# One VectorE sum moved behind four folding operations, ahead of the first output pair of a state-space plus gated-MLP kernel

## The chip, the cores and the metric

The kernel runs on one core of one Trainium2 chip. The time is device microseconds of one execution, and the figure of a kernel is the median over its runs. The core's engines work side by side, each through its own queue of instructions in order: TensorE (PE for its matmuls, PEld for its weight loads), VectorE (DVE), ScalarE (ACT), GpSimd (POOL) and SyncE (SP, which here only issues transfers). An instruction waits at the head of its queue until what it needs is there, and all that stands behind it on that engine waits too.

## The reference

The input `x` is one sequence of 2048 tokens of width 512. It is normalised over its width (`xn`), and two branches read `xn`. Branch A is a diagonal complex state-space layer with 512 states: a projection into the states, a recurrence over all tokens, a projection back, and a skip term. Branch B is a gated MLP with 1792 inner columns. The output is `x` plus both.

```python
xn = layernorm(x)
# A: Bu = xn @ B_bar.T ; h_t = Lam_bar * h_(t-1) + Bu_t
#    y = 2 * Re(h @ C.T) + xn * Dskip
# B: out = (silu(xn @ w1) * (xn @ w3)) @ w2
return x + A(xn) + B(xn)
```

All tensors are bfloat16. Nothing in the change alters what is computed.

## The kernel before

**Tiling.** The 2048 tokens are four blocks of 512. For each block `glu(b)` makes the 14 gate and up products of the MLP (L525), ScalarE takes them out of PSUM (L534, L535), VectorE multiplies them (L543); `bu(b)` makes the inputs of the recurrence (L435), and `ssm_tasks(b)` turns, scans and turns back the states on VectorE (L457 to L488), with two additions per half done by accumulating transfers that GpSimd issues (L468, L492). All of it lands in one activation tile per block, `act`.

**Output pairs.** The last product, `act` by the stacked weights `w2` and `C`, is done for two 128-token chunks at a time, in `y_fast(n)`, n from 0 to 7. Each pair is a two-by-two block product of seven multiplications in place of eight (Strassen's scheme in Winograd's form), so that sums of blocks are needed beforehand: of the activations, `S1 = a21 + a22`, `S3 = a11 - a21` (in place of a21) and `S2 = S1 - a11`, made by `row_sums` (all on L683), and `S4 = a12 - S2`, made inside `y_fast` (L766); of the weights, the eight differences of `weight_sums` (L662), made once.

**PE's order in a pair.** Seven groups of 11 matmuls, all on L724: a11, then S1, then a12, then S2, then a22, then S4, then S3. S4 overwrites a12, so L766 waits for the third group, and the sixth group waits for L766.

**Where the sums lie.** For the pairs 0, 2, 4 and 6, S1 goes over the storage of `x_blk[0]` and S2 over that of `x_blk[1]` (`sum_homes`). So S1 has to wait until block 0 of `x` is no longer read, and S2 until block 1 is no longer read. The last reader of `x_blk[b]` is a transfer: `res_tasks(b)` multiplies `xn_blk[b]` by the skip vector (L622) and then has GpSimd issue an accumulating transfer `xn_blk[b] += x_blk[b]` (L626).

**C's folding.** `weight_c(pt)` multiplies the complex C by the discretisation factor, for four groups of states. Groups 0 and 1 end with one subtraction on VectorE (L400). Groups 2 and 3 end with two fused operations each (L397), which read products that ScalarE made shortly before (L386). The weight differences (L662) read the folded C.

**What sets VectorE's order.** The background work of VectorE is a list, `bg`, a `Filler`. `bg.add(cost, fn, key)` appends a task; `fill`, called after each group of matmuls while the program is written out, takes tasks from the front as long as an estimated VectorE time stays near an estimated PE time; `flush(key)` takes tasks until the last one with that key is out. The order in the list is the order in VectorE's queue, with the gate products (L543) set in between. The list ahead of the first pair is written at L812 to L825: residual of block 0, three weight differences, residual of block 1, folding of groups 0 and 1, a difference of the residual (L634), the three row sums, folding of groups 2 and 3, five weight differences. `ssm_tasks(1)` then adds the turning of block 1, and `y_fast(0)` begins after `glu(1)`.

**After the first pair.** `y_fast(1)` follows at once, and then `glu(2)`, whose matmuls need `xnT` of block 2. That is made by ScalarE (sums L269, squares L275, normalisation L285) with three small steps on GpSimd between them (L272; L278 to L280), and four transposing transfers that SP issues (L242).

Of the kernel before, what the change touches and what calls it, by code (L numbers as in the profile page):

```python
# [63 lines left out]
def kernel(  # L64
# [141 lines left out]
    bg = Filler(LEAD)  # L206
# [207 lines left out]
    def act(b):  # L414
        if act_blk[b] is None:
            act_blk[b] = actp.tile([P, 2 * NK, TBLK], FP16, name="act")
        return act_blk[b]
# [213 lines left out]
    def res_difference(b):  # L631
        def difference():
            o = xn_blk[b]
            nc.vector.tensor_tensor(out=o[:, 0::2, D2].bitcast(FP16), in0=o[:, 0::2, D2], in1=o[:, 1::2, D2],  # L634
                                    op=ALU.subtract)

        bg.add(0.4, difference, ("res", b))
# [38 lines left out]
    def row_sums(n, b, p):  # L676
        a = act(b)
        r1, r2 = slice(2 * p * P, (2 * p + 1) * P), slice((2 * p + 1) * P, (2 * p + 2) * P)
        a11, a12 = a[:, 0:NK, r1], a[:, NK:2 * NK, r1]
        a21, a22 = a[:, 0:NK, r2], a[:, NK:2 * NK, r2]  # L680
        s1, s2 = (v.bitcast(FP16).rearrange("p (k t) -> p k t", t=P) for v in homes[n % 2])
        sums[n] = dict(a11=a11, a12=a12, a22=a22, s1=s1, s2=s2, s3=a21)
        return [(0.9, lambda out=out, x=x, z=z, op=op: nc.vector.tensor_tensor(out=out, in0=x, in1=z, op=op), ("sums", n))  # L683
                for out, x, z, op in ((s1, a21, a22, ALU.add), (a21, a11, a21, ALU.subtract),
                                      (s2, s1, a11, ALU.subtract))]
# [123 lines left out]
    pairs = [(b, p) for b in range(NBLK) for p in range(CPB // 2)]  # L809
# [7 lines left out]
    for fn in finish_c[:2]:  # L817
        bg.add(0.7, fn, "tw")
    res_difference(0)
    for t in row_sums(0, *pairs[0]):  # L820
        bg.add(*t)
    for fn in finish_c[2:]:
        bg.add(1.4, fn, "tw")
    for i, which in ((0, 3), (1, 2), (1, 0), (1, 1), (1, 3)):
        weight_sum(i, which)  # L825

# [70 lines left out]
```

## Time and profile before

| What | Value |
|---|---|
| median of 8 runs | 206.22 us (205.59 to 207.2) |
| the profiled execution: its time | 205.59 us |
| the profiled execution: its span | 203.8 us, so 1.8 us lie around the span |
| PE granted clock, whole span | 0.999 |
| VectorE busy, 61.2 to 63.1 us | 0.02 us of 1.9 |
| PE busy, 60 to 70 us | 9.95 us of 10 |
| PE busy, 70 to 77 us | 6.15 us of 7 |
| PE busy, 77 to 88 us | 10.83 us of 11 |
| L626 for block 1 | issued at 58.12 us, landed 5.0 us later |
| L626, all four | 4.5 to 6.4 us from issue to landing |

Times in the profile count from the start of the span. A row of the timeline gives the start, the length, the engine, the line, the operation and its operands; in square brackets stands how long the engine had been idle and what ended the idle time. Consecutive VectorE operations overlap by some 0.08 us, so that the step from one start to the next is a little shorter than the length shown. The chain of waits follows the work that ended last backwards: a piece of PE in it is time in which PE was the limit, a piece of VectorE is time in which PE's next work hung on VectorE.

### The profile page before, as it was taken

Reading aid. Unit: us, or ns where it says so; the run is one execution under the profiler, and the core shown is the slowest. Engines: PE = TensorE matmul, PEld = TensorE weight load, DVE = VectorE, ACT = ScalarE, POOL = GpSimd, SP = SyncE. Lnnn points to the kernel's source line nnn. Section 1 sums busy time; section 2 is a strip of 40 time slices with the busy share of each in tenths; the row PEclk is TensorE's granted clock in tenths of the full one; section 3 lists DMA queues with packets and bytes.
Section 4 is the critical chain, followed back from the end, with each engine's and each line's share of the span. In section 5 each row is a group of like instructions: output and inputs, shape, how many; then the busy total and the mean of one; then the engine's idle time right before and its main releaser. Section 6 shows DMA issues by size and latency. Waiting matters only on the chain.

```text
span 203.8 us, 3431 instructions
## 1 busy us (share of the span) xinstructions
PE 197.9 (97%) x1304; PEld 122.5 (60%) x1317; DVE 172.6 (85%) x242; ACT 125.0 (61%) x251; POOL 41.7 (20%) x65
## 2 busy tenths in 40 slices
PE   8999999999999998999999999999999999999994
PEld 2774444444444587854444445888444458888993
DVE  3789699999996999999959999999999935684932
ACT  4699797799999966588876676210566672101010
POOL 3250279600310141434111010310101210000000
PEclk9999999999999999999999999999999999999999
DMA  6998994991672015844796105476240790101011
GB/s 167 271 278 193 329 158 102 332 279 37 123 149 40 0 37 97 156 126 91 94 179 132 26 0 106 83 150 132 77 77 0 142 169 2 51 3 51 26 43 39
DMA packets 28696, 23.16 MB, mean 114 GB/s; under 512 B 16008, under 2 KB 26376, under 8 KB 28680
## 3 DMA queue, kind: packets, MB, share of 16 engines
q1 hardware_dynamic: 25512, 13.21, 26.5%
q0 software_dynamic: 2592, 9.44, 24.8%
q10 hardware_dynamic: 576, 0.30, 0.5%
q8 instruction: 10, 0.16, 0.3%
q14 instruction: 6, 0.05, 0.1%
HBM read 7.74 MB, written 2.10 MB: 48 GB/s over the span
## 4 chain that ended last, share of the span: by engine, by line
PE 86%; DVE 7%; DMA 4%; issue 0%; ACTq 0%; ACT 0%
PE gu_ps L525 41%; PE gu_ps L724 16%; PE y_ps L724 8%; PE y_ps L435 7%; PE bu_ps L435 7%; PE bu_ps L724 6%; DMA w_sb<-in_B_w_dram 2%; DMA x_blk<-in_A_x_dram 1%; DVE tw L662 1%; DVE ct L397 1%; DVE act L543 1%; DVE p L457 1%; PE gu_ps L557 1%; PE bu_ps L557 1%; DVE u L461 1%; DVE xn L735 1%
## 5 line engine op out<-in xcount | busy, mean ns | idle before, releaser
L525 PE MATMUL gu_ps<-xnT,w_sb 128*128 128x512 bf16 x415 | 91.9, 379 | 0.5
L525 PEld LDWEIGHTS <-w_sb 128*128 128x128 bf16 x424 | 41.5, 98 | 49.4
L724 PEld LDWEIGHTS <-act 128*128 128x128 f16 x451 | 43.2, 98 | 6.8 <-DVE act L766 1.3
L534 ACT ACTIVATE g<-gu_ps 128x512 bf16<-128x512 f32 x55 | 33.1, 601 | 13.2 <-PE gu_ps L525 12.9
L535 ACT ACTIVATE u<-gu_ps 128x512 bf16<-128x512 f32 x55 | 33.2, 603 | 9.6 <-PE gu_ps L525 9.2
L543 DVE TENSOR_TENSOR act<-g,u 128x1024 f16<-128x1024 bf16 x28 | 19.0, 678 | 3.9 <-ACT u L535 3.9
L435 PEld LDWEIGHTS <-bt 128*128 128x128 bf16 x128 | 12.5, 98 | 15.1
L478 DVE TENSOR_TENSOR_SCAN u<-rho,act,u 128x512 bf16<-128x512 f32 x16 | 19.6, 1268 | 0.0
L492 POOL DMA_DIRECT2D act<-p x8 | 7.2, 900 | 42.2 <-DVE act L488 28.2
L435 PE MATMUL y_ps<-xnT,bt 128*128 128x512 bf16 x63 | 15.1, 379 | 0.1
L435 PE MATMUL bu_ps<-xnT,bt 128*128 128x512 bf16 x61 | 14.8, 379 | 0.1
L457 DVE TENSOR_TENSOR p<-u,tabe 128x2048 bf16<-128x2048 bf16 x8 | 9.8, 1221 | 2.6 <-DMA act<-p 2.5
L468 POOL DMA_DIRECT2D u<-p x6 | 5.3, 878 | 30.0 <-DVE u L461 9.9
L724 PE MATMUL y_ps<-tw,act 128*128 128x256 f16 x88 | 10.9, 273 | 0.0
L724 PE MATMUL gu_ps<-w_sb,act 128*128 128x256 bf16 (+1 forms) x84 | 10.8, 268 | 0.0
L724 PE MATMUL gu_ps<-tw,act 128*128 128x256 f16 x88 | 10.7, 273 | 0.0
L437 ACT ACTIVATE u<-bu_ps 128x512 bf16<-128x512 f32 x16 | 9.4, 597 | 2.0 <-PE bu_ps L435 1.6
L437 ACT ACTIVATE u<-y_ps 128x512 bf16<-128x512 f32 x16 | 9.5, 596 | 1.8 <-PE y_ps L435 1.3
L461 DVE TENSOR_TENSOR u<-u,tabe 128x2048 bf16<-128x2048 bf16 x8 | 9.8, 1222 | 0.2
L744 ACT ACTIVATE bu_ps<-y_ps 128x256 f32<-128x256 f32 x4 | 1.5, 369 | 13.7 <-PE y_ps L724 13.7
L478 DVE TENSOR_TENSOR_SCAN u<-rho,ends,u 128x512 bf16<-128x512 f32 x8 | 9.9, 1267 | 0.0
L484 DVE TENSOR_TENSOR p<-u,tabe 128x2048 f16<-128x2048 bf16 x8 | 9.8, 1222 | 0.1
(143 smaller groups left out, 277.2 us busy)
## 6 DMA issues: line engine op xcount, KB each, us to landing
act<-p POOLq DMA_DIRECT2D x8, 512.0 KB, 4.8
u<-p POOLq DMA_DIRECT2D x6, 512.0 KB, 4.7
xn<-x_blk POOLq DMA_DIRECT2D x4, 512.0 KB, 5.5
out_dram<-xn SPq DMA_DIRECT2D x15, 128.0 KB, 1.7
w_sb<-in_B_w_dram SPq DMA_DIRECT2D x1, 1792.0 KB
x_blk<-in_A_x_dram SPq DMA_DIRECT2D x3, 512.0 KB, 9.3
w_sb<-in_B_w_dram SPq DMA_DIRECT2D x2, 768.0 KB, 6.8
w_sb<-in_B_w_dram SPq DMA_DIRECT2D x4, 256.0 KB, 4.2
```

The source lines that it names most:

```text
L435: nc.tensor.matmul(out=ps, lhsT=bt[:, ri, dt, pt * P:(pt + 1) * P], rhs=xnT_blk[b][:, dt, :], start=(dt == 0), stop=(dt == NDT - 1))
L437: nc.scalar.activation(out=u[:, j, ri, :], in_=ps, func=ACT.Copy)
L457: nc.vector.tensor_tensor(out=st["p"][:, :, ::-1, :], in0=st["g"], in1=tabe[:, psl, 2:0:-1, :], op=ALU.mult)
L461: nc.vector.tensor_tensor(out=st["g"], in0=st["g"], in1=tabe[:, psl, 0:1, :].to_broadcast(FULL), op=ALU.mult)
L478: nc.vector.tensor_tensor_scan(out=v, data0=rho[:, pt:pt + 1].to_broadcast([P, TBLK]), data1=v, initial=init, op0=ALU.mult, op1=ALU.add)
L484: nc.vector.tensor_tensor(out=st["p16"][:, :, ::-1, :], in0=st["g"], in1=tabe[:, psl, 1:3, :], op=ALU.mult)
L492: gp.dma_start(out=act_state(b, hf), in_=st["p16"], accum_op=ALU.add)
L525: nc.tensor.matmul(out=ps[:, tsl], lhsT=w[:, dt, f * P:(f + 1) * P], rhs=xnT[:, dt, tsl], start=(dt == 0), stop=(dt == NDT - 1))
L534: nc.scalar.activation(out=g16[:, f % 2, :], in_=g_ps, func=ACT.Silu)
L535: nc.scalar.activation(out=u16[:, f % 2, :], in_=u_ps, func=ACT.Copy)
L543: nc.vector.tensor_tensor(out=act(b)[:, k0:k1 + 1:k1 - k0, :], in0=g16, in1=u16, op=ALU.mult)
L724: nc.tensor.matmul(out=out, lhsT=left[:, k, :], rhs=right[k][:, cols], start=(start and k == 0), stop=(k == NK - 1), skip_group_check=True)
```

## The change

The third row sum, S2, is added to the list after the folding of groups 2 and 3, and not before it. S1 and S3 keep their place. In VectorE's queue the four L397 operations move ahead of the last L683 operation of pair 0; the queues of the other four engines hold the same instructions in the same order.

```diff
     for fn in finish_c[:2]:
         bg.add(0.7, fn, "tw")
     res_difference(0)
-    for t in row_sums(0, *pairs[0]):
+    first_sums = row_sums(0, *pairs[0])
+    for t in first_sums[:2]:
         bg.add(*t)
     for fn in finish_c[2:]:
         bg.add(1.4, fn, "tw")
+    bg.add(*first_sums[2])
     for i, which in ((0, 3), (1, 2), (1, 0), (1, 1), (1, 3)):
         weight_sum(i, which)
```

## The prediction

> **What bounds the kernel now.** I read the engine totals first, then the chain of waits, then the waits of VectorE and PE in the stretch that the diff touches, and last the timelines there.
>
> ```profile
> PE 197.9 (97%) x1304; PEld 122.5 (60%) x1317; DVE 172.6 (85%) x242; ACT 125.0 (61%) x251; POOL 41.7 (20%) x65
> ```
>
> PE is busy 97% of the span, so a change on another engine counts only where PE stands still for it. The chain shows one such place after the start-up:
>
> ```profile
> 63.90 2.73 DVE ct L397 x4
> 66.64 1.00 DVE tw L662
> ...
> 75.63 0.60 DVE act L543
> 76.23 0.08 DVE ends L833
> 76.31 0.81 DVE act L766
> 77.12 0.05 issue
> 77.17 1.38 PE bu_ps L724 x11
> 78.54 1.20 PE y_ps L724 x11
> 79.74 8.41 PE gu_ps L724 x77
> ```
>
> From 63.90 to 77.12 the chain runs through VectorE alone, one operation after the other, and ends in L766, which makes S4 for the first pair; then it is PE's again, and from 77.17 on it stays with PE until 199.58. PE's own rows show what the wait cost it:
>
> ```profile
> 73.58 1.36 PE L724 MATMUL y_ps<-tw,x_blk 128*128 128x256 f16 x11
> 74.78 1.36 PE L724 MATMUL y_ps<-tw,act 128*128 128x256 f16 x11
> 77.17 0.94 PE L724 MATMUL bu_ps<-w_sb,act 128*128 128x256 bf16 x7 [1.02 <-DVE act L766]
> ```
>
> A group of 11 takes 74.78 - 73.58 = 1.20 us, so the sixth group was due at 74.78 + 1.20 = 75.98 and began at 77.17: PE lost 1.19 us. (The idle figure of 1.02 counts from the modelled end of the last matmul.) VectorE, which was late there, had itself stood still once:
>
> ```profile
> 60.32 0.89 DVE L683 TENSOR_TENSOR act<-act 128x1408 f16<-128x1408 f16 x1
> 63.09 0.89 DVE L683 TENSOR_TENSOR x_blk<-x_blk,act 128x1408 f16<-128x1408 f16 x1 [1.88 <-DMA xn<-x_blk]
> 63.90 2.73 DVE L397 SCALAR_TENSOR_TENSOR ct<-ct,w2c,tw 128x512 f16<-128x512 bf16 x4
> 66.55 1.09 DVE L662 TENSOR_TENSOR tw<-w_sb,tw 128x1792 f16<-128x1792 bf16 x1
> ```
>
> S2 (63.09) waited 1.88 us for the transfer `xn += x` of block 1, which still read the storage that S2 takes. No other VectorE wait lies between 40 and 90 us, so this idle time arrives whole at L766.
>
> **The change part by part.** No instruction is added or removed. Four L397 operations pass one L683; no queue of PE, ACT, POOL or SP changes.
>
> *The L397 operations, earlier.* S3 starts at 60.32 and the next start could follow 0.81 us later (the step from 63.09 to 63.90), at 61.13. What must be there: the products of ScalarE, whose last L386 starts at 60.31 and takes 0.71, so ends at 61.02 for the last of them, and for the third and fourth L397 only; and `w2c`, long made. No wait. The four take 66.55 - 63.90 = 2.65 us and end at 63.78.
>
> *S2, later.* The transfer was issued at 58.12 and let S2 start at 63.09. Nothing ahead of its issue changes. At 63.78 it has landed, with 0.69 us to spare. S2 then takes 0.81 and L662, at 66.55 before, starts at 64.59: VectorE is 1.96 us earlier. Bounds for the landing from the four L626 rows, 4.5 to 6.4 us after issue: 62.6 to 64.5. At the late end S2 waits 0.7 us and VectorE is 1.2 us earlier. I take the row of this very transfer, 63.09.
>
> *From L662 to L766.* Thirteen operations that follow each other with hardly a gap now. Each could meet a new wait once it comes 1.96 us earlier. Of the four gate products L543 the first was made ready before 60 us; those at 70.21, 73.81 and 75.55 need ScalarE's L535, which end at 63.87, 67.33 and 70.78; they would start at 68.25, 71.85 and 73.59: no wait. L766 needs PE's third group, whose last matmuls start at 73.15 and run 0.60, to 73.75; it would start at 76.23 - 1.96 = 74.27: no wait, 0.5 us to spare. It would end at 77.11 - 1.96 = 75.15, ahead of PE's due time of 75.98. So PE's wait goes altogether, and the gain there is the smaller of 1.96 and 1.19: **1.19 us**. Were VectorE only 1.2 us earlier, it would still be about 1.2.
>
> *What is late next.* Two things. First, `glu(2)`: PE comes to it at 87.98 - 1.19 = 86.79, and needs all four transposes of block 2. SP issues the fourth at 82.82 and is held until 84.57; its 256-byte packets end at about 87.2. Between 84 and 86 the transfers of the software queue alone moved (48 and 50 packets, the accumulation L468 that GpSimd issued at 82.06); the transposes' packets came after it, 435 of the hardware queue from 86 to 87.
>
> ```profile
> 82.06 0.93 POOL L468 DMA_DIRECT2D u<-p  x1 [4.64 <-DVE u L461]
> 82.82 1.75 SPq L242 DMA_TRANSPOSE xnT<-xn  x1
> 87.98 2.32 PE L525 MATMUL gu_ps<-xnT,w_sb 128*128 128x512 bf16 x9
> ```
>
> Both chains move. GpSimd's L278 began at 75.16, behind an L468 of VectorE's making (74.19 to 75.08); that L468 comes 1.9 us earlier, and then ScalarE's last sum, at 74.15, decides: L278 starts about 0.95 us earlier, and so do L279, L280, L285 and the transposes. The second L468 hangs on VectorE and comes 1.9 us earlier: its packets, 83.5 to 86.7 before, lie at 81.6 to 84.8 and now meet the third transpose too. If third and fourth both follow the accumulation, with about 0.9 us of packets each (as the third had, 82.5 to 83.5) they end near 84.8 + 1.8 = 86.6; unhindered the fourth would end about 84.4 (2.5 us from issue, like the second and third, at 81.87). Both are before 86.79. I take no wait; the bounds are 0 and 0.4 us (nothing of the chain moves, 87.2).
>
> The DMA page of the Trainium skill (DMA: Bandwidth & Descriptors, Queues, rings and completion order) says that an engine takes its queues in turn, packet by packet; the rows from 84 to 86 show one queue alone. By the rule the transposes end near 84.4 to 85, by the rows near 86.6, and the sum is the same.
>
> A rule against the change is in the page SBUF — State Buffer (Who interferes with whom): a VectorE instruction with two SBUF inputs and a GpSimd instruction that reads SBUF block each other. L278 to L280 move under other VectorE operations; here they took 0.53, 1.37 and 0.20 us, the same steps for block 3 took 0.79, 2.09 and 0.21. With the longer rows the transposes gain nothing, the fourth ends near 87.2 and 0.4 of the 1.19 is lost.
>
> Second, pair 2: its L766 runs from 130.88 to 131.76, and PE's sixth group begins at 131.97. That margin is 0.2 us. It stays, since VectorE is tied to PE again at 88.19, where its addition of pair 1 waits for PE's last group: in the first pairs VectorE may run 1.96 ahead, but from there on both are 1.19 earlier.
>
> *Sum.* Span 203.8 - 1.19 = 202.6; with the 1.8 us around it the profiled execution goes from 205.59 to 204.4. That execution was the fastest of the eight; the median is 0.63 above it, so I set the gain against the median: 206.22 - 1.2 = **205.0 us**. Own range of this case, 204.5 to 205.5: the gain between 0.7 and 1.7, the upper end because PE may have lost more in the slower runs.
>
> **The rivals.**
>
> *A, transposes late.* The wait removed comes back in part at `glu(2)`: 0.4 us if the last transpose still ends at 87.2. For it: the accumulation now covers two transposes. Against it: the chain ahead of them starts earlier. 206.22 - 0.8 = 205.4.
>
> *B, the change doesn't do what it says.* S2 still waits, because the transfer lands late in most runs. Half the gain is left if VectorE is only 0.6 us earlier, that is a landing at about 65.1, 7.0 us after issue. Against it: the L626 rows end at 6.4. For it: one accumulation of this size (L492 at 38.3) took 9.4. 206.22 - 0.6 = 205.6; with none left 206.2.
>
> *C, slower.* Place: the first matmul of `glu(2)`. Third and fourth transpose both stand still until the accumulation ends at 84.8 and then run one after the other at the longest unhindered time of issue to landing, 2.9 us each: 90.6, a wait of 3.8 in place of 1.19, so 206.22 + 2.6 = 208.8. It is slower by more than 0.3% from a landing at 86.79 + 1.19 + 0.62 = 88.6 on. Against it: the first three followed each other at 1.3 us, not 2.9.
>
> **How the numbers follow.** My forecast 0.67, A 0.15, B 0.10, C 0.08. The predicted time is the forecast's, 205.0. The range takes in the forecast, A and most of B: 204.3 to 206.1. A measurement of this kernel can tell a change of about 0.3%, 0.62 us, from none. Faster by more: 0.65 from the forecast, 0.09 from A, 0.01 from B, together 0.75. Within: 0.02, 0.06 and 0.08, together 0.16. Slower: C and a part of B, 0.09.
>
> **What would show it.** In the changed profile: the four L397 start near 61.1 with no idle time before them; L683 follows near 63.8 with no wait for the transfer; L766 ends near 75.2; PE's sixth group starts at 76.0 with no idle time; `glu(2)` starts near 86.8. The forecast is wrong if VectorE still waits there by more than 0.7 us, if PE waits before `glu(2)`, or if pair 2's sixth group waits for its L766.

## The result, and the profile after

The changed kernel takes 204.12 us in the median of 11 runs (203.69 to 205.2), against 206.27 us for the kernel before in 32 runs (205.2 to 207.96). The ratio is 0.9901 with a 95% interval of 0.9882 to 0.9920: it is 1.6 to 2.4 us faster, where 1.2 was forecast. The direction and the place were right; the gain came out larger, and the time lies 0.2 us below the range. The profiled execution took 204.66 us with a span of 202.4; the span is 1.4 less than before, the time 0.9 less, since 2.3 us lie around this span and 1.8 lay around that one.

The timeline of VectorE after (start, length, engine, line, operation; an idle time would stand in brackets at the end):

```profile
59.97 0.89 DVE L683 TENSOR_TENSOR act<-act 128x1408 f16<-128x1408 f16 x1
60.78 2.73 DVE L397 SCALAR_TENSOR_TENSOR ct<-ct,w2c,tw 128x512 f16<-128x512 bf16 x4
63.55 0.89 DVE L683 TENSOR_TENSOR x_blk<-x_blk,act 128x1408 f16<-128x1408 f16 x1
64.36 1.08 DVE L662 TENSOR_TENSOR tw<-w_sb,tw 128x1792 f16<-128x1792 bf16 x1
...
74.03 0.88 DVE L766 TENSOR_TENSOR act<-act,x_blk 128x1408 f16<-128x1408 f16 x1
```

The four L397 follow S3 at once, S2 has no bracket, and the step from S3 to L766 is 14.06 us where it was 15.91 (60.32 to 76.23): 1.85 less, forecast 1.96. PE's timeline after:

```profile
73.36 1.36 PE L724 MATMUL y_ps<-tw,x_blk 128*128 128x256 f16 x11
74.56 1.36 PE L724 MATMUL y_ps<-tw,act 128*128 128x256 f16 x11
75.76 0.93 PE L724 MATMUL bu_ps<-w_sb,act 128*128 128x256 bf16 x7
```

The sixth group follows the fifth after 1.20 us, like the fifth the fourth: nothing is lost. L766 ended at 74.91 (74.03 + 0.88), 0.85 us ahead of it. The chain of waits after, in the stretch where it ran through VectorE before:

```profile
67.17 2.75 PE gu_ps L525 x12
69.92 1.20 PE y_ps L724 x11
71.12 2.40 PE bu_ps L724 x22
73.52 2.40 PE y_ps L724 x22
75.92 1.20 PE bu_ps L724 x11
77.12 1.20 PE y_ps L724 x11
78.32 8.41 PE gu_ps L724 x77
86.73 0.22 PE gu_ps L525
```

It is PE's all the way. What is left of VectorE's lead is given back in the second pair, where VectorE now waits for PE (its waits between 63 and 100 us):

```profile
DVE x_blk L735 <- PE gu_ps L724: 0.5, 1, 0.5
DVE act L766 <- PE gu_ps L724: 0.2, 1, 0.2
```

So the 1.85 us of VectorE became 1.19 us of PE, as forecast, and the rest is idle time of VectorE. In this pair of profiles that explains 1.2 of the 1.4 us of span. The medians differ by 2.15, and the experiments are about that difference.

One figure recurs below. PE's first full-width matmul of `glu(0)` (L525) starts between 12.41 and 13.57 us in the profiles, whatever the kernel, where the chain of waits before it runs through the first loads of `x` and the weights. I call the time from there to the end of the span "the rest": it is 190.80 us in the profile before and 189.62 in the profile after, a difference of 1.18, which agrees with PE's 1.19 lost. Spans are shown to 0.1 us, so a rest is known to 0.05. The other 0.22 of the span's 1.4 lies in that start.

### The profile page after: what moved, and what is told of

Same layout as the page of the kernel before. It is cut to its first block, busy times and chain, and to the rows that moved or that the text cites. A ratio compares the mean times of both kernels' runs of the same rounds, so it can differ in the third digit from the quotient of the medians.

```text
span 202.4 us, 3431 instructions
## 1 busy us (share of the span) xinstructions
PE 196.9 (97%) x1304; PEld 122.4 (60%) x1317; DVE 172.7 (85%) x242; ACT 125.4 (62%) x251; POOL 40.3 (20%) x65
## 4 chain that ended last, share of the span: by engine, by line
PE 93%; DMA 2%; SPq 2%; DVE 1%; issue 1%
PE gu_ps L525 45%; PE gu_ps L724 16%; PE y_ps L724 9%; PE bu_ps L724 7%; PE y_ps L435 7%; PE bu_ps L435 7%; DMA w_sb<-in_B_w_dram 2%; PE gu_ps L557 1%; PE bu_ps L557 1%; DVE xn L735 1%; SPq L166 0%; SPq L151 0%; SPq L161 0%; SPq L152 0%; DVE x_blk L735 0%
## 5 line engine op out<-in xcount | busy, mean ns | idle before, releaser
L525 PE MATMUL gu_ps<-xnT,w_sb 128*128 128x512 bf16 x415 | 91.9, 379 | 0.5
L525 PEld LDWEIGHTS <-w_sb 128*128 128x128 bf16 x424 | 41.4, 98 | 49.4
L484 DVE TENSOR_TENSOR p<-u,tabe 128x2048 f16<-128x2048 bf16 x8 | 9.8, 1220 | 0.1
```

The costliest lines, as they stand in the source:

```text
L484: nc.vector.tensor_tensor(out=st["p16"][:, :, ::-1, :], in0=st["g"], in1=tabe[:, psl, 1:3, :], op=ALU.mult)
L525: nc.tensor.matmul(out=ps[:, tsl], lhsT=w[:, dt, f * P:(f + 1) * P], rhs=xnT[:, dt, tsl], start=(dt == 0), stop=(dt == NDT - 1))
```

## The experiments

Theory 1: PE loses more to the wait in most runs than in the one profile of before, and the wait is the whole cause. Theory 2: the wait costs 1.2 us, and the order brings something elsewhere. Later expectations name two more. All kernels of one batch share a chip and the runs of the kernel before on it.

### The kernel before, profiled again

No edit. What was expected of the first two:

> The kernel before, unchanged, profiled once more. Theory 1 (the wait is longer in most runs than in the one profile of before, since the transfer of L626 for block 1 lands later): S2 on L683 waits 2.3 to 4 us in place of 1.88, the landing is 5.5 to 7 us after issue in place of 5.0, and PE's sixth group of the first pair starts 1.6 to 3 us late in place of 1.19. Theory 2 (the wait in that profile is typical, and the rest of the 2.15 us is won elsewhere): wait 1.7 to 2.1 us, sixth group 1.0 to 1.4 us late, and a second place where PE stands still that the first profile does not have.

> The kernel before, unchanged, a third profile. Theory 1: wait at S2 2.3 to 4 us, the sixth group of the first pair 1.6 to 3 us late. Theory 2: wait 1.7 to 2.1 us, sixth group 1.0 to 1.4 us late.

Waiting row and PE row of the first of them:

```profile
63.16 0.89 DVE L683 TENSOR_TENSOR x_blk<-x_blk,act 128x1408 f16<-128x1408 f16 x1 [2.49 <-DMA xn<-x_blk]
...
77.23 0.94 PE L724 MATMUL bu_ps<-w_sb,act 128*128 128x256 bf16 x7 [1.52 <-DVE act L766]
```

Together with two more looks on another chip (their expectations stand further down) and the profile of the prediction:

| Profile of before | landing of L626 after issue | S2 waits | sixth group late | `glu(2)` late | the rest |
|---|---|---|---|---|---|
| the one forecast from | 5.0 | 1.88 | 1.19 | 0.00 | 190.80 |
| look_before_1 | 5.5 | 2.49 | 1.69 | 0.01 | 191.34 |
| look_before_2 | 5.2 | 2.04 | 1.38 | 0.14 | 191.13 |
| look_before_3 | 5.1 | 2.19 | 1.38 | 0.23 | 191.19 |
| look_before_4 | 5.2 | 2.08 | 1.43 | 0.00 | 191.05 |

(Microseconds; late is the start of the sixth group less the start of the fifth less 1.20, and the start of `glu(2)` less the start of the last group of the second pair less 1.20.) In all five the sixth group starts 14.07 or 14.08 us after S2 does (63.16 and 77.23 above), so what S2 loses to the landing PE loses one for one. Theory 1 has the direction, though of the four only look_before_1 reaches the sizes that it first named, and look_before_2 lies within theory 2's: the profile forecast from had the earliest landing, the shortest wait and the smallest loss of the five. The mean loss is 1.41 us.

Theory 2 needs a second place where PE stands still. There is one in two of the five, at the start of `glu(2)`, where the weight loads wait for a transpose of block 2. In look_before_3:

```profile
86.39 1.36 PE L724 MATMUL gu_ps<-tw,act 128*128 128x256 f16 x11
87.82 2.55 PE L525 MATMUL gu_ps<-xnT,w_sb 128*128 128x512 bf16 x10
87.82 2.27 PEld L525 LDWEIGHTS <-w_sb 128*128 128x128 bf16 x12 [0.35 <-DMA xnT<-xn]
```

The mean over the five is 0.08 us, so it explains little of the 2.15. It is absent in the three profiles of the changed kernel and in the three without the transfer below.

### The cause taken away: no transfer to wait for

```diff
         def add():
-            gp.dma_start(out=xn_blk[b], in_=x_blk[b], accum_op=ALU.add)
+            if b != 1:
+                gp.dma_start(out=xn_blk[b], in_=x_blk[b], accum_op=ALU.add)
```

In the order of before, and so with nothing for S2 to wait for.

> Order of before, without the accumulating transfer of block 1 (the output of block 1 lacks x). So S2 has nothing to wait for, and the order of VectorE is as it was. Theory 1: all of the gain comes from this wait, so the time is that of the changed kernel, 204.1 (203.7 to 204.6), ratio to before 0.988 to 0.992. Theory 2: only 1.2 us, 205.1 (204.8 to 205.4), ratio 0.993 to 0.996.

204.37 us against 205.75 of before on that chip (ratio 0.9931, 0.9905 to 0.9956): 1.4 us. The times that the expectation names, 204.1 and 205.1, come from the first measurement, so I compare the ratio: it lies above theory 1's band (0.988 to 0.992) and just inside theory 2's. By itself this run does not decide between them; the next ones on one chip do. Its rest is 189.59 us, that of the changed kernel within the 0.05 to which it is known. S2 follows S3 at once in the old order:

```profile
60.75 0.89 DVE L684 TENSOR_TENSOR act<-act 128x1408 f16<-128x1408 f16 x1
61.56 0.88 DVE L684 TENSOR_TENSOR x_blk<-x_blk,act 128x1408 f16<-128x1408 f16 x1
62.36 2.73 DVE L397 SCALAR_TENSOR_TENSOR ct<-ct,w2c,tw 128x512 f16<-128x512 bf16 x4
```

### The lead given back by fixed work

The changed kernel, with six small additions behind S2 (their target is overwritten before it is read):

```diff
     bg.add(*first_sums[2])
+    room = x_blk[0].rearrange("p c d -> p (c d)").bitcast(FP16)
+    for _ in range(6):
+        bg.add(0.0, lambda: nc.vector.tensor_tensor(out=room[:, NK * P:NK * P + D], in0=room[:, 0:D], in1=room[:, D:2 * D], op=ALU.add), "tw")
```

> Order of after, with six additions of 512 elements on VectorE behind S2, some 0.33 us each, so that VectorE reaches L766 2.0 us later by a fixed amount and not by a wait for a transfer. L766 ends 0.9 us ahead of PE's need in the profile of after, so 2.0 - 0.9 = 1.1 us come back. Theory 1: 204.1 + 1.1 = 205.2 (204.9 to 205.6), a full us below before, since the wait in before is longer than 2 us in most runs; sixth group 1.0 to 1.3 us late. Theory 2: what hangs on VectorE's lead elsewhere is lost too, so 205.8 to 206.4.

206.46 us, ratio 1.0029 (1.0002 to 1.0056): hardly slower than before, but 0.9 us above the 205.6 at which theory 1's band ends, so that expectation missed. VectorE's timeline, and then PE's waits between 60 and 143 us:

```profile
64.78 2.71 DVE L828 TENSOR_TENSOR x_blk<-x_blk 128x512 f16<-128x512 f16 x6
```

```profile
PE bu_ps L724 <- DVE act L766: 1.8, 1, 1.8
PE gu_ps L525 <- DMA xnT<-xn: 0.2, 1, 0.2
```

The six take 2.63 us (64.78 to 67.41), not 2.0. PE's sixth group is 1.92 us late, that is 2.63 less 0.71: what L766 has to spare goes first, and the remainder reaches PE. The second line of the waits is the place of rival A of the prediction: PE waits for a transpose of block 2, and `glu(2)` starts 1.55 us after the last group of the second pair where the pace is 1.20, so 0.35 late. Together 2.3 us, as much as the rest grew (191.88 against 189.6); the time is 2.1 above the 204.37 that `no_add` takes on this chip. It is just above theory 2's band, but by the profile this is VectorE's lateness and no second effect of the order.

### The change and the missing transfer on one chip

Four kernels on one chip. `no_add_and_order` has both edits.

> The changed kernel once more, beside the next three and the same runs of before. Theory 1 (the wait for the transfer is the whole cause; PE lost 1.19, 1.69 and 1.38 us to it in the three profiles of before, mean 1.42): 1.2 to 1.7 us faster than before, ratio 0.992 to 0.994, below the 2.15 us of the first measurement, and within 0.3 us of the kernel without the transfer. Theory 2 (the order itself brings 0.6 us more): ratio 0.988 to 0.991 again, and 0.5 us or more below the kernel without the transfer.

> Order of before, without the accumulating transfer of block 1 (the output of block 1 lacks x). Theory 1: ratio 0.992 to 0.994, within 0.3 us of the changed kernel. Theory 2: ratio 0.992 to 0.995, but 0.5 us or more above the changed kernel.

> Order of after, and without the accumulating transfer of block 1 (the output of block 1 lacks x): the change with nothing left to avoid. Theory 1: the order is worth nothing once the wait is gone, so the time is that of the two kernels before it within 0.3 us. Theory 2: 0.5 us or more below the kernel without the transfer in the old order. If S2 still waits in many runs of the changed kernel by more than the 0.9 us that L766 has to spare, this one is faster than the changed kernel.

| Kernel (before: 205.63) | median us | ratio, 95% interval | the rest |
|---|---|---|---|
| after_again | 204.43 | 0.9937, 0.9914 to 0.9960 | 189.55 |
| no_add_again | 204.33 | 0.9934, 0.9908 to 0.9960 | 189.56 |
| no_add_and_order | 204.53 | 0.9938, 0.9915 to 0.9961 | 189.56 |

All three are within 0.2 us, where theory 2 needed 0.5, and their rests agree within the 0.05 to which they are known. So the order is worth what the wait cost and nothing more, and the changed kernel hides all of the wait: theory 2 falls. The gain here is 1.2 us.

### Another way to the same end

Order of before, but the residual of block 1 ahead of the weight differences, so that the transfer is issued earlier:

```diff
     res_tasks(0)
+    res_tasks(1)
     for which in (2, 0, 1):
         weight_sum(0, which)
-    res_tasks(1)
```

> Order of before, but the residual of block 1 (L622, and the transfer of L626) stands ahead of the three weight differences and not behind them: the same work, the transfer issued some 3.5 us earlier. It queues behind the accumulation of block 0, whose packets end at 58.5 in the first profile, and takes 3.2 us of packets, so it should land at about 62 in place of 63.1, and S2 still waits some 0.8 us. Theory 1: VectorE is 1.1 to 1.5 us earlier at L766, PE loses 0 to 0.3 us, and the time is within 0.4 us of the changed kernel, ratio 0.992 to 0.995. Theory 2: 0.6 us or more above the changed kernel.

```profile
62.01 0.89 DVE L683 TENSOR_TENSOR x_blk<-x_blk,act 128x1408 f16<-128x1408 f16 x1 [0.99 <-DMA xn<-x_blk]
```

The transfer did as expected: issued at 54.31, landed 7.7 us later behind the accumulation of block 0, S2 waits 0.99 us, and PE's sixth group is 0.17 late, 14.07 us after S2 once more. The time, 205.0 us (0.9970, 0.9944 to 0.9996), is 0.57 above after_again: it missed the 0.4 that was allowed and the ratio of 0.992 to 0.995, and nearly reaches theory 2's 0.6. The rest is 189.97, 0.4 above after_again, and the profile shows where the second part of it goes: to the start of `glu(2)`, 0.23 late (1.43 us after the group before it), where PE's weight loads again wait 0.3 us for a transpose.

```profile
85.69 1.36 PE L724 MATMUL gu_ps<-tw,act 128*128 128x256 f16 x11
87.12 3.20 PE L525 MATMUL gu_ps<-xnT,w_sb 128*128 128x512 bf16 x13
```

That leaves 0.2 us; the runs spread from 204.43 to 207.14, and a longer wait of S2 in some of them would do it, but it isn't shown. The new order is the better way.

### A third chip

> The changed kernel on whatever chip comes. Theory 1 (the gain is what PE lost to the wait, 1.19, 1.69 and 1.38 us in three profiles, and no more): ratio 0.992 to 0.994, and from the first matmul of L525 to the end of the span 189.5 to 189.7 us, as in the two profiles of it so far. Theory 3 (on some chips the transfer lands later, so that before loses 2 us there and after nothing): ratio 0.989 to 0.991 where the two profiles of before beside it show a landing of 5.8 us or more after issue, and 0.992 to 0.995 where they show 5.0 to 5.5.

> The kernel before, unchanged, profiled on the chip of the run above. Theory 1: landing 5.0 to 5.5 us after issue, sixth group of the first pair 1.2 to 1.7 us late, 190.8 to 191.3 us from the first matmul of L525 to the end of the span. Theory 3: landing 5.8 us or more and the group 1.9 us late or more, if the ratio above is 0.991 or less.

> The kernel before, unchanged, profiled once more on the same chip. Theory 1: landing 5.0 to 5.5 us after issue, sixth group 1.2 to 1.7 us late. Theory 3: as in the look before it.

204.32 against 205.87 us, ratio 0.9932 (0.9907 to 0.9957), 1.55 us; the rest is 189.55. The two looks at before are in the table above: landings of 5.1 and 5.2, groups 1.38 and 1.43 late. Theory 1 holds for this chip. Theory 3 could not be tried by it, since the ratio stayed above 0.991.

### A later transfer, made on purpose

To see what a later landing costs in either order, the residual of block 1 was put behind the two L400; the second kernel has the same edit in the changed one.

```diff
-    res_tasks(1)
     ln_alloc(2)
     for fn in finish_c[:2]:
         bg.add(0.7, fn, "tw")
+    res_tasks(1)
```

> Order of before, but the residual of block 1 (L622 and the transfer of L626) stands behind the folding of groups 0 and 1 (two L400), so that the transfer is issued 1.3 us later; the same work. Theory 3 (before pays for a later landing one for one, which is why one set of runs can show 2 us and others 1.3): S2 starts 1.2 to 1.4 us later, the sixth group of the first pair is 2.4 to 3.1 us late in place of 1.2 to 1.7, 192.2 to 192.6 us from the first L525 to the end, ratio to before 1.005 to 1.008. Theory 4 (the wait is covered by something else beyond some point): less than half of it, ratio below 1.003.

> The same later transfer with the order of after. Theory 3: S2 now waits for the landing 0.8 to 1.4 us behind the four L397, of which L766 has 0.7 to 0.9 us to spare, so PE's sixth group is 0 to 0.6 us late and the time 0 to 0.6 us above the changed kernel: 189.6 to 190.2 us from the first L525 to the end, ratio to before 0.993 to 0.996, and about 2.2 us (1.9 to 2.6) below the kernel with the later transfer in the old order. Theory 4: the gap between the two is 1.4 us as between after and before.

Old order, then new order:

```profile
63.92 0.89 DVE L683 TENSOR_TENSOR x_blk<-x_blk,act 128x1408 f16<-128x1408 f16 x1 [2.57 <-DMA xn<-x_blk]
...
77.99 0.94 PE L724 MATMUL bu_ps<-w_sb,act 128*128 128x256 bf16 x7 [1.98 <-DVE act L766]
```

```profile
61.33 2.73 DVE L397 SCALAR_TENSOR_TENSOR ct<-ct,w2c,tw 128x512 f16<-128x512 bf16 x4
64.17 0.89 DVE L683 TENSOR_TENSOR x_blk<-x_blk,act 128x1408 f16<-128x1408 f16 x1
...
76.32 0.93 PE L724 MATMUL bu_ps<-w_sb,act 128*128 128x256 bf16 x7
```

In the old order the group is 2.15 us late and the rest 192.10; the time is 206.64 against 205.96 (1.0032, 1.0007 to 1.0057). All of these fall short of theory 3's bands, and the ratio is hardly above theory 4's 1.003. The step is smaller than expected because the transfer landed 4.5 us after issue in place of 5.0 to 5.5. In this profile it was issued not 1.3 but 1.6 us later, since L484 had waited 0.3 us for another transfer before; counted from the first L525, S2 started 0.9 us later than in the mean of the five profiles of before. The sixth group still follows S2 after 14.07 us, so nothing covers the wait, which theory 4 needs. In the new order S2 starts 0.2 us after the last L397 would let it, which costs PE nothing: the rest is 189.56, and the time is 204.46 (0.9919, 0.9890 to 0.9948), a little better than expected. The two orders lie 2.2 us apart in the medians, as theory 3 said, and not 1.4. So the gain grows with the landing: the old order pays for it and the new one doesn't.

## Why the prediction was right in its steps and wrong in its number

- **The place and the chain of cause.** Right, and shown: one wait of S2 for the transfer, passed on to L766 and PE's sixth group. Without the transfer the old order is as fast as the new one, and both together are no faster than either.
- **L397 without a wait, S2 without a wait.** Right in all three profiles of the changed kernel. The 0.69 us to spare was not there in the profile after: the landing came 5.6 us after issue, and S2 started at 63.55, some 0.1 us after the last L397 let it. That costs PE nothing, because L766 has 0.85 us to spare.
- **1.19 us for PE.** This is the term that was mis-sized. I took the loss in the one profile as the loss of the median run. That profile had the smallest of five, which run from 1.19 to 1.69 with a mean of 1.41, and the 0.08 us at `glu(2)` that the change also takes away did not show in it; the rest falls from a mean of 191.1 us (five profiles of before) to 189.6 (three of after), 1.5 us. I had noted that this execution was the fastest of the eight, and used it only to widen the range by 0.5 us. With 1.5 in place of 1.2 the sum gives 204.7 us, still within the range: this term accounts for 0.3 us of the miss of 0.9, and not for the whole.
- **Setting the gain against 206.22.** In four other batches, on four chips, the medians of before were 205.75, 205.63, 205.87 and 205.96; in two of them the changed kernel ran, with 204.43 and 204.32. Where both ran in one batch the gain was 1.20 and 1.55 us, as the profiles say. The first measurement shows 2.15, some 0.6 to 0.9 more. Of this, 0.3 to 0.6 lies in a slower kernel before (206.27) and 0.2 to 0.3 in a faster kernel after (204.12). Later landings in that set could do the first: the profile after from it has the latest of the unedited kernels, 5.6 us, and the last experiment shows a 2.2 us gain where the transfer comes late. They can't do the second, since the changed kernel doesn't wait. But no profile of before with such a loss was caught, and the start alone moves by up to 1.2 us from profile to profile. Chance is not excluded either: the intervals of the three gains (1.6 to 2.4, 0.8 to 1.8, 0.9 to 1.9 us) overlap. This part stays open.
- **What is late next.** The transposes moved ahead with VectorE as worked out: GpSimd's L278 started at 74.03 (forecast 0.95 earlier than 75.16, so 74.2), the packets of the fourth transpose ended at 85.6, between the 84.4 and 86.6 that were worked out, and `glu(2)` started at 86.57 without a wait. Only the fourth ran into the accumulation, not the third too. GpSimd's three steps took 0.94, 1.05 and 0.26 us, a sum of 2.25 against 2.10 before (2.32 and 2.12 in the other two profiles of after). The rule of the Trainium skill that spoke against the change (SBUF — State Buffer, Who interferes with whom) may be in these 0.02 to 0.22 us, which no run shows apart. Its other rule (DMA: Bandwidth & Descriptors, Queues, rings and completion order: queues are served in turn) fits the profile after only in part: from 83 to 84 us the hardware queue moved 40 packets, 0.01 MB, beside 48 of the software queue, 0.20 MB, and the bulk of the fourth transpose came after. Pair 2 kept its margin: L766 ended at 130.35, 0.21 ahead of the group at 130.56.
- **The rivals.** A did not occur in the changed kernel: `glu(2)` was on time in its three profiles. Its place is real, though, where S2 waits or VectorE is late: 0.14 and 0.23 us in two profiles of before, 0.23 in `early_transfer` and `late_transfer`, 0.35 in `pad_6`. The forecast counted nothing there because the one profile showed nothing. B and C did not occur.

## What to carry to other kernels

When an engine waits for a transfer, look at what stands behind it in its queue: independent work that is already fed can go in front, and the wait is paid with work that had to be done anyway. The gain was not the length of the wait (1.88 us) but what the bounding engine lost to it (1.19 in the same profile), so follow it to that engine before counting it. And a wait that ends with a transfer has a spread: profile it several times before a number is taken from it, since a single profile gives a single landing, and a good order is worth most in the runs where the transfer is late.

## What was not expected of the hardware

- The accumulating transfer of 512 KB landed 5.0 to 5.6 us after issue at the same place of the program (nine profiles), and 4.5 us where it was issued 1.3 us later (two). In the profile after one of its parts is behind the others. Its transfers between 62.3 and 63.4 us, when the other parts had ended by 62.2:

```profile
DMA packets 3, 0.01 MB, mean 7 GB/s; under 512 B 1, under 2 KB 1, under 8 KB 3
```

Three packets of 144 are left, the last of them a packet of 4 bytes at 63.17. The landing came after it, at 63.5, so the last part set it. Why one part is late isn't shown.

- Six equal additions of 512 elements that write the same place one after the other ran 0.46 us apart, where the step from the sixth to the next operation, which writes elsewhere, was 0.34 (as was the one behind L634 in the profile before, 59.06 to 59.40). That each of the six waits for the one before is my reading of this; no run shows it apart.
